# The sums of the second product: who forms them, and in which order the seven products run

## The chip, the cores and the metric

The kernel runs on one core of one Trainium2 chip. The metric is device time in microseconds (us), the median of 13 runs. A core has five engines that run side by side, each through its own queue in order: TensorE (PE in the profile; its weight loads are PEld), VectorE (DVE), ScalarE (ACT), GpSimd (POOL) and SyncE (SP), which here only issues DMAs. They wait for each other through semaphores. TensorE writes its results to PSUM, in banks of 128 x 512 float32.

## The reference

Two layers in a row. First an attention with masks: 8 batches, 8 heads, 576 positions, head size 64. Heads 0 to 3 see the last 32 positions, heads 4 to 7 every 32nd one. Its output, 4608 tokens of 512 numbers, goes through a feed-forward layer with a leaky activation:

```python
h = x @ w_in                       # 512 -> 2048
g = np.maximum(h, 0.0) + alpha * np.minimum(h, 0.0)
return (g @ w_out).astype(np.float32)   # 2048 -> 512
```

## The kernel before, in words

**Chunks.** The feed-forward part runs in 9 chunks of 512 tokens (`n` = 0 to 8, `NCH` = 9). The attention of batch n+1 is cut into pieces that are woven into chunk n: transposes of q and k (T), scores (S), the product with v (P, "pv"), and transposes of the result (X). Chunks 1 to 6 carry such pieces, 7 and 8 none. Everything is issued in an order written out by hand (`keep`), so an engine's queue is the order of the code.

**A chunk** has 30 slots (loop at L929). Slots 0 to 15 are the first layer: `lin1_piece` multiplies x by 128 columns of w_in (4 matmuls of 512 columns) into one of three PSUM banks (`hbank`), ScalarE forms the negative part (L647), and VectorE finishes the activation into `gT` (L650, called through the list `late` in the next attention step). A bank is free again once L650 has read it. The pieces alternate: 0, 8, 1, 9 and so on. Slots 16 to 29 are the second layer, `lin2_sums` with i = 0 to 13. After each slot `attn_n` issues as many attention pieces as an accumulator (`acc`) says.

**The second layer** of chunks 1 to 8 uses Strassen's scheme in Winograd's form. g (512 tokens x 2048) and w_out are cut into quadrants; in place of eight block products there are seven, of sums of quadrants. The sums of w_out (`wsum`, and one quadrant of `wout16` overwritten in place) are formed once by `w_sums` (L682). The sums of g are formed per chunk by `g_sum` (L696):

- g1 = quad(1,0) + quad(1,1); g2 = g1 - quad(0,0); g4 = quad(0,1) - g2; g3 = quad(0,0) - quad(1,0), written over quad(1,0) in place.

g1 is formed by GpSimd in three parts of 128 x 512 while the first layer runs (L933), its last part and all others by VectorE at i = 0, 1 and 2. quad(i, j) takes the tokens' half i and the rows 8j to 8j+7 of `gT`, so quad(0,0) and quad(1,0) need pieces 0 to 7 and the other two 8 to 15.

The seven products go into three banks A, B, C. Product p takes slots i = 2p and 2p + 1, one for each half of the tokens, with 8 matmuls of 256 columns in each. In order: A (quad(0,0)), B (g1), A (g2, added to what A holds), B (g4), A (g3), C (quad(0,1)), A (quad(1,1)). After some of them ScalarE copies a bank to SBUF (k1, k5, k2, L763) or VectorE adds a bank and such a copy (L766): o12 = B + k2 after the fourth, o22 = A + k5 after the fifth, o11 = C + k1 after the sixth; o21 is A after the seventh. Each is stored by a DMA on SP's queue (L714).

**Other queues.** GpSimd multiplies the masks into the scores (L427, L434), casts inputs (L196) and issues loads. SP issues stores, loads of q and k, and transposing DMAs: x to xT (L489, L487), and, once per batch, q and k of the strided heads (L141), which the scores of those heads wait for.

**Before chunk 1**, chunk 0's second layer is plain (`lin2_piece`, L664). At its slot 9 VectorE forms the first two sums of w_out and GpSimd the last; GpSimd forms the third after the loop (L694).

Of the kernel before, what the change touches and what calls it, by code (L numbers as in the profile page):

```python
# [9 lines left out]
F32 = mybir.dt.float32  # L10
F16 = mybir.dt.float16
# [20 lines left out]
def kernel(  # L32
# [10 lines left out]
    nc = tc.nc  # L43
# [4 lines left out]
    NCH = NT // 512  # L48
# [5 lines left out]
    cpool = ctx.enter_context(tc.tile_pool(name="const", bufs=1))  # L54
    spool = ctx.enter_context(tc.tile_pool(name="stage", bufs=3))
# [26 lines left out]
    win16 = cpool.tile([128, 4, 2048], F16)  # L82
    wout16 = cpool.tile([128, 16, 512], F16)
    xT = cpool.tile([128, 4, RING], F16)
    gsum = [cpool.tile([128, 8, 256], F16, name=f"gsum{i}") for i in range(3)]
    wsum = [cpool.tile([128, 8, 256], F16, name=f"wsum{i}") for i in range(3)]
    banks = [phpool.tile([128, 512], F32, tag=f"hb{i}", name=f"hb{i}") for i in range(3)]
    turn, busy = [0, 1], []
# [585 lines left out]
    def quad(t, i, j):  # L674

        return t[:, 8 * j : 8 * j + 8, 256 * i : 256 * i + 256]

    def wq(i, j):

        return wout16[:, 8 * i : 8 * i + 8, 256 * j : 256 * j + 256]  # L680

    def w_sums(eng, which):  # L682

        w1, w2, w4 = wsum
        w3 = wq(0, 1)
        steps = {
            1: (w1, wq(0, 1), wq(0, 0), ALU.subtract),
            2: (w2, wq(1, 1), w1, ALU.subtract),
            3: (w3, wq(1, 1), wq(0, 1), ALU.subtract),
            4: (w4, wq(1, 0), w2, ALU.subtract),  # L690
        }
        for z in which:
            o, x, y, op = steps[z]
            keep(eng.tensor_tensor(o, x, y, op=op))  # L694

    def g_sum(eng, n, which, k0, k1):  # L696

        g = gTs[n]
        g1, g2, g4 = gsum
        g3 = quad(g, 1, 0)  # L700
        o, x, y, op = {
            1: (g1, quad(g, 1, 0), quad(g, 1, 1), ALU.add),
            2: (g2, g1, quad(g, 0, 0), ALU.subtract),
            3: (g3, quad(g, 0, 0), quad(g, 1, 0), ALU.subtract),
            4: (g4, quad(g, 0, 1), g2, ALU.subtract),
        }[which]
        keep(eng.tensor_tensor(o[:, k0:k1], x[:, k0:k1], y[:, k0:k1], op=op))  # L707
# [3 lines left out]
    def store(n, i, j, osb, mts=(0, 1)):  # L711
# [3 lines left out]
            out[r0 : r0 + 128 * len(mts), 256 * j : 256 * j + 256].rearrange("(m p) c -> p m c", p=128),  # L715
            osb[:, mts[0] : mts[-1] + 1]))

    def lin2_sums(n, i):

        g = gTs[n]  # L720
        last = n == NCH - 1
        p, mt = i // 2, i % 2
        if i == 0:
            tiles = [banks[z] for z in turn]
            lay.clear()
            for nm, t in zip("ABC", tiles):
                lay[nm] = [t[:, 0:256], t[:, 256:512]]
                lay[nm + "f"] = t
            turn[:] = [turn[1], turn[2], turn[0]]
            if last:  # L730
                lay["A"][1] = pspool.tile([128, 512], F32, tag="ps", name="opl")[:, 0:256]
            g_sum(nc.vector, n, 1, 6, 8)
            g_sum(nc.vector, n, 2, 0, 4)
            g_sum(nc.vector, n, 2, 4, 8)
        if i == 1:
            g_sum(nc.vector, n, 4, 0, 8)
        if i == 2:
            g_sum(nc.vector, n, 3, 0, 8)
        bank, lhs, rhs, first = (
            ("A", quad(g, 0, 0), wq(0, 0), True),  # L740
            ("B", gsum[0], wsum[0], True),
            ("A", gsum[1], wsum[1], False),
            ("B", gsum[2], wq(1, 1), False),
            ("A", quad(g, 1, 0), wq(0, 1), False),
            ("C", quad(g, 0, 1), wq(1, 0), True),
            ("A", quad(g, 1, 1), wsum[2], False),
        )[p]
        dst = lay[bank][mt]
        own = mt == 0 or (last and bank == "A")
        for kf in range(8):  # L750
            keep(nc.tensor.matmul(  # L751
                dst, lhs[:, kf, 128 * mt : 128 * mt + 128], rhs[:, kf, :],
                start=(first and own and kf == 0), stop=(kf == 7), skip_group_check=True))

        def each(fn, o, *more):

            if last and bank == "A":
                fn(o[:, mt], lay["A"][mt], *[z[:, mt] for z in more])
            elif mt == 1:
                fn(o, lay[bank + "f"].rearrange("p (m c) -> p m c", m=2), *more)  # L760

        def act(o, x):
            keep(nc.scalar.copy(o, x))  # L763

        def add(o, x, y):
            keep(nc.vector.tensor_tensor(o, x, y, op=ALU.add))  # L766

        def new(nm):
            if mt == 0:
                held[nm] = (kpool if nm[0] == "k" else opool).tile(  # L770
                    [128, 2, 256], F32, tag=nm if nm[0] == "k" else "osb", name=nm)
            return held[nm]

        if p == 0:
            each(act, new("k1"))
        elif p == 1:
            each(act, new("k5"))
        elif p == 2:
            each(act, new("k2"))
        elif p == 3:  # L780
            each(add, new("o12"), held["k2"])
            if mt:
                store(n, 0, 1, held["o12"])
        elif p == 4:
            each(add, new("o22"), held["k5"])
            if mt:
                store(n, 1, 1, held["o22"])
        elif p == 5:
            each(add, new("o11"), held["k1"])
            if mt:  # L790
                store(n, 0, 0, held["o11"])
        else:
            o21 = new("o21")
            if last and mt:
                keep(nc.vector.tensor_copy(o21[:, 1], lay["A"][1]))
            else:
                each(act, o21)
            if last:
                store(n, 1, 0, o21, (mt,))
            elif mt:  # L800
                store(n, 1, 0, o21)
# [14 lines left out]
            keep(nc.tensor.matmul(wps, wrm[:, 0:128], wrm, start=True, stop=True))  # L816


    wrm = cpool.tile([128, 512], F16)
    wps = banks[2]  # L820
    def load_unit(b, strided, v_too=True):
        load_qk(b, strided, "q")
# [87 lines left out]
        attn_n(0, end1)  # L910
    for i in range(16):
        lin2_piece(0, i)
        if i == 9:
            w_sums(nc.vector, (1, 2))
            w_sums(nc.gpsimd, (4,))
        attn_n(0 if i < 1 else 2 if i < 9 else 1, end1)
    while pos["i"] < end1:
        attn_step(end1)
    wide["on"] = False
    w_sums(nc.gpsimd, (3,))  # L920
    load_unit(3, False)


    for n in range(1, NCH):
        ab = attn_until(n + 1) if n + 1 < B else len(pieces)
        left = ab - pos["i"]
        skip = 4 if n == 1 else 0
        acc = 0.0
        for i in range(30):  # L929
            if i < 16:  # L930
                lin1_piece(n, 8 * (i % 2) + i // 2)
                if i in (3, 7, 11):
                    late.append(lambda i=i: g_sum(nc.gpsimd, n, 1, i // 2 - 1, i // 2 + 1))  # L933
            else:
                lin2_sums(n, i - 16)
            if i >= skip:
                acc += left / ((19 if n == B - 2 else 20.5) - 0.5 * skip) * (0.5 if i < 16 else 1.0)
            cnt = int(acc)
            acc -= cnt
            attn_n(cnt, ab)  # L940
        while pos["i"] < ab:
            attn_step(ab)
# [30 lines left out]
```

## Time and profile before

| | |
|---|---|
| median of 13 runs | 330.66 us (326.71 to 334.95) |
| profiled execution, its own time | 330.84 us |
| its span, first to last instruction | 329.0 us |
| granted TensorE clock | 0.99 |
| PE, DVE, ACT, POOL busy | 307.0, 232.3, 174.6, 181.4 us |
| g_sum on GpSimd (L707), 128x512 | 24 times, 1.15 us each |
| g_sum on VectorE, 128x512 / 128x1024 / 128x2048 | 0.43 / 0.68 / 1.21 us as a rule |
| w_sums (L694), 128x2048, VectorE / GpSimd | 1.21 / 4.05 us |

The page gives for each engine its busy time and its share of the span. Matmuls are pipelined, so their durations overlap: the time of a stretch is read from the start of one group to the start of the next. A row of the timeline has the start in us, the duration, the engine, the line of the code, the operation, output and inputs, how many, and in brackets the idle time before it and what ended it.

### The profile page before, as it was taken

How to read it: one execution, taken by the hardware profiler on the slowest of the kernel's cores; microseconds unless marked ns; L12 is line 12 of the kernel's file. 1: busy time of each engine (PE TensorE's matmuls, PEld its weight loads, DVE VectorE, ACT ScalarE, POOL GpSimd, SP SyncE). 2: the span in 40 equal slices, each digit the busy share in tenths (PEclk: the TensorE clock that was granted, in tenths of full speed). 3: DMA queues.
4: the chain of work that ended last, by engine and by line, in shares of the span. 5: the costliest groups of instructions: out<-in, count | busy, mean ns of one | idle time of the engine just before them, and what ended most of it. 6: DMA issues, size and time to landing. Idle time of an engine off the chain costs nothing.

```text
span 329.0 us, 7189 instructions
## 1 busy us (share of the span) xinstructions
PE 307.0 (93%) x2861; PEld 200.6 (61%) x2861; DVE 232.3 (71%) x420; ACT 174.6 (53%) x325; POOL 181.4 (55%) x180
## 2 busy tenths in 40 slices
PE   7699989999779999999999999999999999999995
PEld 2265446555457546854688878646864685486484
DVE  5356864757797688658875887488748995865872
ACT  1375655458434775377527753775367607624630
POOL 8672388198996975587558744974345401200400
PEclk9799999999899999999999999999999999999999
DMA  7999999949855997399729992997180122003003
GB/s 216 200 206 207 241 184 124 137 149 178 190 78 94 181 213 94 72 210 185 93 53 138 252 111 53 120 162 90 39 191 18 21 55 95 0 12 119 0 2 128
DMA packets 81569, 40.38 MB, mean 123 GB/s; under 512 B 58480, under 2 KB 77184, under 8 KB 81536
## 3 DMA queue, kind: packets, MB, share of 16 engines
q0 software_dynamic: 41728, 17.38, 47.3%
q1 hardware_dynamic: 39808, 22.55, 30.2%
q8 instruction: 22, 0.36, 0.5%
q14 instruction: 11, 0.09, 0.1%
HBM read 38.01 MB, written 9.44 MB: 144 GB/s over the span
## 4 chain that ended last, share of the span: by engine, by line
PE 51%; DVE 21%; DMA 12%; ACT 7%; issue 4%; POOL 2%; SPq 1%; ACTq 0%
PE hb L637 21%; PE hb L751 15%; DMA kT<-ksd 10%; DVE gT L650 6%; DVE gsum L707 5%; PE hb L664 4%; DMA kl<-in_k_dram 3%; DVE qT L194 2%; DVE x L464 2%; DVE gT L707 2%; PE pv L455 2%; ACT neg L647 2%; DVE x16s L464 2%; PE hb L816 2%; DVE rc L462 1%
## 5 line engine op out<-in xcount | busy, mean ns | idle before, releaser
L650 DVE SCALAR_TENSOR_TENSOR gT<-neg,oma,hb 128x512 f16<-128x512 f32 x144 | 105.3, 744 | 40.1 <-ACT neg L647 33.3
L637 PE MATMUL hb<-xT,win 128*128 128x512 f16 (+1 forms) x640 | 132.7, 358 | 0.7
L647 ACT ACTIVATE neg<-hb 128x512 f32<-128x512 f32 x144 | 86.0, 598 | 42.4 <-PE hb L637 40.5
L637 PEld LDWEIGHTS <-win 128*128 128x128 f16 x640 | 60.1, 98 | 56.3 <-issue 2.6
L707 POOL TENSOR_TENSOR gsum<-gT 128x512 f16<-128x512 f16 x24 | 27.7, 1153 | 63.9 <-DVE gT L650 63.6
L427 POOL TENSOR_TENSOR et<-et,consts 128x576 f16<-128x576 f16 (+1 forms) x24 | 31.9, 1331 | 39.6 <-ACT et L425 39.6
L751 PEld LDWEIGHTS <-gT 128*128 128x128 f16 x512 | 48.0, 99 | 9.1 <-DVE gT L650 1.6
L751 PE MATMUL hb<-wout,gT 128*128 128x256 f16 x368 | 47.6, 278 | 0.5
L751 PEld LDWEIGHTS <-gsum 128*128 128x128 f16 x384 | 35.6, 97 | 6.7 <-DVE gsum L707 1.9
L464 DVE TENSOR_TENSOR x<-pv,rc 96x384 f16<-96x384 f32 (+2 forms) x62 | 33.0, 532 | 2.1
L434 POOL TENSOR_TENSOR et<-et,consts 128x576 f16<-128x576 f16 (+1 forms) x24 | 31.4, 1309 | 0.7 <-ACT et L431 0.6
L751 PE MATMUL hb<-wsum,gsum 128*128 128x256 f16 x248 | 30.7, 273 | 1.2 <-DVE gsum L707 1.2
L455 PEld LDWEIGHTS <-et 72*128 72x128 f16 (+1 forms) x448 | 24.2, 98 | 11.2 <-POOL et L434 2.7
L462 DVE RECIPROCAL rc<-pv 72x6 f32<-72x6 f32 (+2 forms) x80 | 14.6, 182 | 22.5 <-PE pv L455 22.5
L766 DVE TENSOR_TENSOR o<-hb,k 128x512 f32<-128x512 f32 (+1 forms) x24 | 16.3, 679 | 15.4 <-PE hb L751 11.6
L425 ACT ACTIVATE et<-sp 128x576 f16<-128x576 f32 (+1 forms) x24 | 15.7, 652 | 21.3 <-PE sp L412 21.1
L763 ACT COPY k<-hb 128x512 f32<-128x512 f32 (+1 forms) x24 | 13.3, 572 | 21.4 <-PE hb L751 21.4
L431 ACT ACTIVATE et<-sph 128x288 f16<-128x288 f32 (+1 forms) x48 | 18.3, 413 | 0.9 <-PE sph L412 0.9
L816 PE MATMUL hb<-wrm 128*128 128x512 f16 x44 | 17.1, 466 | 1.2 <-DVE wrm L828 1.2
L751 PE MATMUL hb<-wout,gsum 128*128 128x256 f16 x128 | 16.2, 272 | 0.8 <-ACT k L763 0.8
L664 PE MATMUL hb<-wout,gT 128*128 128x512 f16 x64 | 16.3, 379 | 0.1
L455 PE MATMUL pv<-vs,et 72*128 72x65 f16 x256 | 15.4, 193 | 0.2 <-DVE x16s L464 0.2
(109 smaller groups left out, 339.4 us busy)
## 6 DMA issues: line engine op xcount, KB each, us to landing
out_dram<-o SPq DMA_DIRECT2D x31, 256.0 KB, 3.0
ql<-in_q_dram SPq DMA_DIRECT2D x6, 512.0 KB, 6.5
kl<-in_k_dram SPq DMA_DIRECT2D x6, 512.0 KB, 8.0
stv<-in_v_dram POOLq DMA_DIRECT2D x8, 288.0 KB, 7.5
vl<-in_v_dram POOLq DMA_DIRECT2D x6, 384.0 KB, 10.9
win<-in_moe_w_in_dram POOLq DMA_DIRECT2D x4, 512.0 KB, 9.3
wout<-in_moe_w_out_dram POOLq DMA_DIRECT2D x4, 512.0 KB, 13.3
qsd<-in_q_dram POOLq DMA_DIRECT2D x6, 288.0 KB, 5.8
```

The source lines that it names most:

```text
L427: keep(nc.gpsimd.tensor_tensor(mv, mv, m, op=ALU.mult))
L431: keep(nc.scalar.activation(ev[:, n * y : n * y + n], sps[y][0:r, 0:n], AF.Exp, scale=SCALE))
L434: keep(nc.gpsimd.tensor_tensor(mv, mv, m, op=ALU.mult))
L455: keep(nc.tensor.matmul(pv[:, 65 * x : 65 * x + 65], et[0:r, c : c + 128], v16[0:r, 2 * P.pr + hh, t, :] if P.strided else v16[:, 6 * (2 * ...
L464: keep(nc.vector.tensor_tensor(P.x16[0:w, c0 : c0 + 64 * nb].rearrange("r (c e) -> r c e", e=64), pvv[:, :, 0:64], rc[0:w, 0:nb].unsqueeze ...
L637: keep(nc.tensor.matmul(hps[:, dst : dst + w], win16[:, kk, 128 * m : 128 * m + 128], xT[:, kk, src : src + w], start=(kk == 0 and x == 0) ...
L647: keep(nc.scalar.activation(neg, hps, AF.Relu, scale=-1.0))
L650: keep(nc.vector.scalar_tensor_tensor(gTs[n][:, m, :], neg, oma[:, m : m + 1], hps, op0=ALU.mult, op1=ALU.add))
L664: keep(nc.tensor.matmul(ops, gTs[n][:, kf, 128 * mt : 128 * mt + 128], wout16[:, kf, :], start=(kf == 0), stop=(kf == 15)))
L707: keep(eng.tensor_tensor(o[:, k0:k1], x[:, k0:k1], y[:, k0:k1], op=op))
L751: keep(nc.tensor.matmul(dst, lhs[:, kf, 128 * mt : 128 * mt + 128], rhs[:, kf, :], start=(first and own and kf == 0), stop=(kf == 7), skip ...
L816: keep(nc.tensor.matmul(wps, wrm[:, 0:128], wrm, start=True, stop=True))
```

## The change

It has a function `quiet(n)`, true for chunks 7 and 8, which keep the old order. In chunks 1 to 6:

- lin1 pieces run in natural order 0 to 15.
- g3 gets a tile of its own (a fourth `gsum`) and is formed in lin1 slots 10 and 12, in two parts of 128 x 1024, by GpSimd (in chunk 1 by VectorE).
- g1 and g2 are each one VectorE instruction of 128 x 2048 at i = 0; g4 is one at i = 4.
- The product order is p = (0, 5, 1, 2, 3, 4, 6): the product into C comes second. Copies, adds and stores follow their product. The banks for the next chunk are handed over as C, B, A.
- If slot 27 would get no attention piece, it gets one.

For all chunks: weight sums 1, 2, 4 are on VectorE in slots 9, 11, 13 of chunk 0, and weight sum 3 on VectorE in lin1 slot 6 of chunk 1. To make room in SBUF, k1 shares k2's buffer (in chunks 7 and 8 the staging buffer of v), and the operand of the warm-up matmuls is a part of the first `gsum`.

```diff
@@ g_sum
-        g1, g2, g4 = gsum
-        g3 = quad(g, 1, 0)
+        g1, g2, g4, g3 = gsum
...
+    def quiet(n):
+        return n >= NCH - 2
@@ lin2_sums
-            turn[:] = [turn[1], turn[2], turn[0]]
+            turn[:] = [turn[1], turn[2], turn[0]] if quiet(n) else [turn[2], turn[1], turn[0]]
...
-            g_sum(nc.vector, n, 1, 6, 8)
-            g_sum(nc.vector, n, 2, 0, 4)
-            g_sum(nc.vector, n, 2, 4, 8)
-        if i == 1:
+            if quiet(n):
+                g_sum(nc.vector, n, 1, 6, 8)
+                g_sum(nc.vector, n, 2, 0, 4)
+                g_sum(nc.vector, n, 2, 4, 8)
+            else:
+                g_sum(nc.vector, n, 1, 0, 8)
+                g_sum(nc.vector, n, 2, 0, 8)
+        if i == (1 if quiet(n) else 4):
             g_sum(nc.vector, n, 4, 0, 8)
-        if i == 2:
+        if i == 2 and quiet(n):
             g_sum(nc.vector, n, 3, 0, 8)
+        p = (p if quiet(n) else (0, 5, 1, 2, 3, 4, 6)[p])
...
-            ("A", quad(g, 1, 0), wq(0, 1), False),
+            ("A", gsum[3], wq(0, 1), False),
...
+                if nm == "k1":
+                    pool, tag = (spool, "v") if quiet(n) else (kpool, "k2")
@@ chunk 0's second layer
-        if i == 9:
-            w_sums(nc.vector, (1, 2))
-            w_sums(nc.gpsimd, (4,))
+        if i in (9, 11, 13):
+            w_sums(nc.vector, ({9: 1, 11: 2, 13: 4}[i],))
...
-    w_sums(nc.gpsimd, (3,))
@@ the loop over chunks
-                lin1_piece(n, 8 * (i % 2) + i // 2)
-                if i in (3, 7, 11):
-                    late.append(lambda i=i: g_sum(nc.gpsimd, n, 1, i // 2 - 1, i // 2 + 1))
+                if quiet(n):
+                    lin1_piece(n, 8 * (i % 2) + i // 2)
+                    if i in (3, 7, 11):
+                        late.append(lambda i=i: g_sum(nc.gpsimd, n, 1, i // 2 - 1, i // 2 + 1))
+                else:
+                    lin1_piece(n, i)
+                    if i in (10, 12):
+                        g_sum(nc.vector if n == 1 else nc.gpsimd, n, 3, 2 * i - 20, 2 * i - 16)
+                if n == 1 and i == 6:
+                    w_sums(nc.vector, (3,))
...
+            if i == 27 and cnt == 0 and pos["i"] < ab:
+                cnt = 1
```

More of the change, by code (lines that the diff above doesn't have):

```diff
@@ L84 @@
     xT = cpool.tile([128, 4, RING], F16)
-    gsum = [cpool.tile([128, 8, 256], F16, name=f"gsum{i}") for i in range(3)]
+    gsum = [cpool.tile([128, 8, 256], F16, name=f"gsum{i}") for i in range(4)]
     wsum = [cpool.tile([128, 8, 256], F16, name=f"wsum{i}") for i in range(3)]
@@ L769, in new @@
             if mt == 0:
-                held[nm] = (kpool if nm[0] == "k" else opool).tile(
-                    [128, 2, 256], F32, tag=nm if nm[0] == "k" else "osb", name=nm)
+                pool, tag = (kpool, nm) if nm[0] == "k" else (opool, "osb")
+                if nm == "k1":
+                    pool, tag = (spool, "v") if quiet(n) else (kpool, "k2")
+                held[nm] = pool.tile([128, 2, 256], F32, tag=tag, name=nm, **({"bufs": 2} if tag == "v" else {}))
             return held[nm]
@@ L816, in warm @@
             keep(nc.tensor.matmul(wps, wrm[:, 0:128], wrm, start=True, stop=True))
-    wrm = cpool.tile([128, 512], F16)
+    wrm = gsum[0].rearrange("p k c -> p (k c)")[:, 0:512]
     wps = banks[2]
```

## The prediction

> **What bounds the kernel now.** I read the engine totals, then the busy time by stage, then the order of work in one stage.
>
> ```profile
> span 329.0 us, 7189 instructions
> PE 307.0 (93%) x2861; PEld 200.6 (61%) x2861; DVE 232.3 (71%) x420; ACT 174.6 (53%) x325; POOL 181.4 (55%) x180
> ...
> 69.00:115.20 46.20, 40.55 (x404) 25.69 (x403) 35.07 (x57) 26.46 (x51) 41.53 (x37) 0.96 0.90 150
> 115.20:148.37 33.17, 31.92 (x317) 21.14 (x316) 24.50 (x46) 19.45 (x37) 22.08 (x21) 1.00 1.03 149
> 148.37:181.74 33.37, 31.95 (x335) 23.08 (x336) 24.92 (x48) 19.47 (x37) 22.30 (x22) 1.00 0.87 120
> ```
>
> The stage rows give length, then PE, PEld, DVE, ACT and POOL busy. TensorE is the bound and the change takes no matmul away, so only its stalls can be won or added. Chunks 2 to 5 take 33.4 us each. Chunk 1 (68.5 to 109.7 in the order of TensorE's work) takes 41.2, with DVE and POOL both loaded. Next, TensorE in chunk 3's second layer, from its first product (slot 0) on:
>
> ```profile
> 159.13 1.35 PE L751 MATMUL hb<-wout,gT 128*128 128x256 f16 x8
> ...
> 162.69 0.61 PE L252 MATMUL tp<-consts,kl 128*128 128x128 f16 x8
> 163.65 0.27 PE L282 MATMUL tt<-consts,tl 128*128 128x128 f16 x2 [0.34 <-DVE qT L194]
> ...
> 166.73 0.58 PE L412 MATMUL sph<-qT,kT 64*128 64x96 f16 x6
> 167.51 1.03 PE L751 MATMUL hb<-wout,gsum 128*128 128x256 f16 x8 [0.20 <-ACT k L763]
> ...
> 172.83 1.05 PE L751 MATMUL hb<-wout,gT 128*128 128x256 f16 x8
> 173.72 0.35 PE L455 MATMUL pv<-vl,et 128*128 128x65 f16 x6
> 173.90 1.04 PE L751 MATMUL hb<-wsum,gT 128*128 128x256 f16 x8
> ...
> 181.30 0.30 PE L412 MATMUL sp<-qT,kT 64*128 64x72 f16 x8 [0.37 <-DMA kT<-ksd]
> ```
>
> A slot's eight matmuls take 0.87 us from start to start. Stalls: 0.3 at slot 0 (waits for gT), 0.5 at the transposes of a tail (the qT copy on DVE is late), 0.55 at the scores after slot 5, 0.37 at the scores that wait for a transposing DMA. VectorE in the same stretch, and in chunk 1:
>
> ```profile
> 160.83 0.43 DVE L707 TENSOR_TENSOR gsum<-gT 128x512 f16<-128x512 f16 x1
> 161.17 1.29 DVE L707 TENSOR_TENSOR gsum<-gsum,gT 128x1024 f16<-128x1024 f16 x2
> 162.37 1.22 DVE L194 COPY qT<-tp 128x1024 f16<-128x1024 f16 x1
> ...
> 173.92 0.69 DVE L766 TENSOR_TENSOR o<-hb,k 128x512 f32<-128x512 f32 x1 [1.52 <-PE hb L751]
> ...
> 88.83 4.32 DVE L707 TENSOR_TENSOR gsum<-gT 128x512 f16<-128x512 f16 x1
> ```
>
> **What the Trainium skill says.** "SBUF — State Buffer", Who interferes with whom: a VectorE instruction with two SBUF inputs and a GpSimd instruction that reads SBUF exclude each other for a whole instruction. The trace agrees: the sum at 88.83 took 4.32 us instead of 0.43, while GpSimd ran masks and casts without a gap to 92.8. "PSUM — Partial Sum Buffer", PSUM bank collisions: two engines may not touch one bank together, so work is ordered by bank. The trace agrees in the tail's bank: ScalarE's kT copy waited 2.36 us for VectorE's qT copy. "GPSIMD Engine Reference", Engine selection: two-input work is about 2 times slower on GpSimd; here 2048 elements take 4.05 against 1.21 us, and that is used.
>
> **Part 1: the turn from the fifth product to the last (slots 10, 11 to 12, 13).** Both use bank A. Before, product C stood between them; now it is second. After slot 11, o22 = A + k5 must be read by VectorE before TensorE writes A again. The last row of TensorE's slot 11 shows the price: matmuls from 172.83, the add at 173.92 for 0.69, so A is free at 174.61, about 174.66 with the 0.05 us of other handovers. TensorE is ready at 173.90. Only the pv piece (0.19) stands between, and it is already in that 173.90. Stall 0.76. It covers the 0.15 us that the next transposes wait for today: +0.6 a chunk in 2 to 5, +0.75 in chunks 1 and 6. The rule at i == 27 adds nothing: by the same accumulator every chunk from 1 to 6 already has a piece in that slot, so attention pieces stay where they are.
>
> **Part 2: start of layer 2, chunks 2 to 5.** Lin1 in natural order makes gT 0 to 7 ready early: slot 0's 0.3 goes. But g1 is now whole on VectorE: two sums of 1.13 (spacing of a 2048-element sum) plus 0.1 stand ahead of the qT copy, 2.4 us instead of 1.6. That copy ends near 164.4, not 163.59, and the tail's transposes wait for its buffer: 0.8 later, and since TensorE arrives 0.3 earlier its wait grows from 0.5 to some 1.5. Then it is given back: g4 leaves slot 1 and g3 leaves VectorE, so the tail copies, which waited behind them until 166.46, are done by 165.1, and the 0.55 at the scores is gone. Following both engines' queues, slot 6 begins at 167.6 instead of 167.51: +0.15 with rounding (bounds -0.4 and +0.6). The second product covers the new g1 and g2, which end at 163.2; they are needed at 165.3 and 167.6. k1 shares k2's buffer: read at slot 3, written again at slot 7.
>
> **Part 3: g3 on GpSimd.** 512 elements cost 1.15, 2048 cost 4.05, so 1024 about 2.1, twice, against 3 x 1.15 before: +0.8 a chunk on an engine busy 22 of 33. Queued behind it: two DMA issues (now ahead of it, 2 us earlier) and the masks of the scores in slot 12. In chunk 3 the masks end at 160.3 instead of 160.0; g1 begins at 160.82. Cost nothing while that 0.5 us margin holds.
>
> **Part 4: SP's queue.** The store of o12 stood ahead of the qT and kT transposing DMAs at 170.42; now o11's, done at slot 3, does, and the transposes start about 1.7 us earlier. Their stalls, 0.45, 0.20, 0.37 and 0.43 in chunks 2 to 5, go: -1.45 in all. The loads of tails and v behind the old weight sums on GpSimd start up to 10 us earlier; nothing waited for them.
>
> **Part 5: chunk 1.** Weight sums 1, 2, 4 on VectorE in slots 9, 11, 13 of chunk 0: 3 x 1.21, hidden, since VectorE idles 1.46 and 1.90 us there. The third, at i == 6, stands ahead of a finish that frees a bank (three banks): +0.75. g3 there is 2 x 0.68 on VectorE beside a GpSimd that runs without a gap from 79.6 to 86.1: nothing if it slips in, 3 us if it starves as at 88.83; I take +0.25. GpSimd's 8.1 us of weight sums were over by 72.3 and it waited 0.72 for ScalarE at 79.6, so the 2.25 us stall for its mask at 86.16 stays. In layer 2 the slot-0 stall of 0.8 goes, but g1 and g2 must still find the lock free: 0.8 later to 0.5 earlier at the tail's transposes; with the gain spent I take the two together as -0.75. Turn +0.75. Sum 0.75 + 0.25 - 0.75 + 0.75 = +1.0, bounds -3.3 and +3.
>
> **Part 6: chunk 6.** No tail. VectorE's sums meet GpSimd's masks (259.71 to 262.4) today and would again; g4, queued after the pv copies, ends near 267.65 for a slot that starts at 267.57: +0.1, and the turn +0.75. Chunks 7 and 8 keep their order; g3 out of place costs the same.
>
> **Sum.** 4 x (0.6 + 0.15) - 1.45 + 1.0 + 0.85 = +3.4 us on the profiled 330.84 (span 329.0, 1.8 around it). The median of the runs is 330.66, so 334.1.
>
> **Rivals.**
> - Not slower: chunk 1's lock stall vanishes, because the order of POOL and DVE there is new. Between 87.86 and 100.38 TensorE spends 12.5 us on 8.2 of work (by starts: seven slots of 0.87, four pv of 0.19, scores 0.36, transposes 0.45 and 0.56); all 4.3 won gives 334.1 - 4.3 = 329.8. It decides once g1 starts at once instead of after 3.9 us. For it: POOL has one sum of 1.15 less there. Against: the masks and casts that held the lock remain.
> - The turn is cheaper: an attention piece runs long or VectorE answers sooner, 0.3 instead of 0.76: -2.7, 331.4. Against: the piece there is 0.19.
> - Masks late in every chunk: GpSimd's sums take 0.5 longer than interpolated, g1 meets the lock and all of layer 2 moves by 1 us in four chunks: 338.
> - The edits don't act (i == 27 indeed does not): excluded for the order of products, which is written out.
>
> **How the numbers follow.** 0.5 for the forecast (332.3 to 336.5), 0.22 for chunk 1's relief (half of it, with other gains, below 329.0), 0.10 for the cheap turn, 0.10 for late masks, 0.08 for relief and cheap turn together (327.5). A difference under 0.5%, 1.65 us, is no change that can be told. Faster 0.11 + 0.08, same 0.11 + 0.10, slower 0.6. Range 328.0 to 338.0; the forecast's own stands above.
>
> **What would show it.** Right: a wait for the add of o22 before the last product in chunks 1 to 6, 0.6 to 0.8 each; no wait for kT's DMA after chunk 1; no 0.3 at slot 0; the tail's transposes waiting about 1.5. Wrong: chunk 1 under 39 us, waits at the turn under 0.4, or a first sum of several us in chunks 2 to 5.

## The result, and the profile after

The changed kernel takes 337.45 us (median of 11 runs, 335.45 to 341.93) against 330.71 (48 runs): 1.0221 of the time before, 95% interval 1.0185 to 1.0258. It is slower, as forecast, but by 6.7 us where 3.4 were forecast. The ratios here and below leave out executions more than 1.5% above the fastest of their kernel; the medians do not.

The head of the page of the changed kernel, and its busy time by chunk (length; then busy time of PE, PEld, DVE, ACT, POOL, each with its instructions; then TensorE's granted clock, DMA share, GB/s):

```profile
span 338.5 us, 7176 instructions
PE 308.5 (91%) x2861; PEld 202.6 (60%) x2861; DVE 240.0 (71%) x412; ACT 174.5 (52%) x325; POOL 173.8 (51%) x170
...
70.94:118.59 47.65, 37.12 (x364) 24.09 (x363) 38.79 (x51) 23.04 (x44) 25.55 (x25) 0.89 0.71 124
118.59:151.82 33.23, 31.41 (x317) 21.14 (x315) 24.61 (x44) 19.45 (x36) 24.58 (x22) 1.00 1.02 145
```

The same rows of the kernel before:

```profile
68.50:109.67 41.17, 35.97 (x364) 23.56 (x363) 31.41 (x50) 23.14 (x44) 37.00 (x32) 0.96 0.86 143
109.67:143.07 33.40, 31.90 (x317) 21.11 (x315) 24.75 (x46) 19.46 (x36) 23.61 (x24) 1.00 1.02 139
```

Chunk 1 grew by 6.5 us, with 7.4 us more of VectorE and 11.5 us less of GpSimd; chunk 2 did not grow. By the starts of TensorE's groups, the chunks compare so (us):

| | before | changed |
|---|---|---|
| start of chunk 1 | 68.48 | 70.94 |
| chunk 1 | 41.19 | 47.65 |
| chunks 2, 3, 4, 5 | 33.40, 33.15, 33.41, 33.38 | 33.23, 33.23, 33.73, 33.23 |
| chunk 6 | 30.19 | 30.70 |
| chunk 7 | 26.06 | 26.06 |

The start of chunk 1 lay anywhere from 64.6 to 72.3 us in the profiled executions of this study, with the same TensorE work before it; so below chunks are compared, not whole profiled times. Each figure by chunk comes from one profiled execution. That of the changed kernel took 340.30 us at a granted clock of 0.97, longer than its median; that of the kernel before took 330.84 at 0.99. From chunk 1 on the profiled execution lost 338.5 - 70.94 less 329.0 - 68.48, which is 7.0 us: 6.5 in chunk 1, 0.1 in chunks 2 to 5 together, 0.5 in chunk 6.

**Where chunk 1 lost it.** (L706, L759, L771 and L774 of the changed kernel are L707, L751, L763 and L766 of the one printed above.) TensorE's timeline in chunk 1 of the changed kernel: the wait for a mask in slot 14, the one for a finish (L650) in slot 15, and the one inside the scores of pair 11, the last two heads of batch 2, whose scores stand behind slot 18 in the second layer:

```profile
89.88 0.36 PE L455 MATMUL pv<-vl,et 128*128 128x65 f16 x6 [2.62 <-POOL et L434]
94.95 1.86 PE L637 MATMUL hb<-xT,win 128*128 128x512 f16 x4 [4.71 <-DVE gT L650]
...
103.38 0.30 PE L412 MATMUL sph<-qT,kT 64*128 64x72 f16 x7 [1.12 <-DVE x L464]
```

What VectorE did then (finishes, then a g3 part, and so on):

```profile
82.92 1.74 DVE L706 TENSOR_TENSOR gsum<-gT 128x1024 f16<-128x1024 f16 x1
84.58 1.39 DVE L650 SCALAR_TENSOR_TENSOR gT<-neg,oma,hb 128x512 f16<-128x512 f32 x2
85.90 7.65 DVE L706 TENSOR_TENSOR gsum<-gT 128x1024 f16<-128x1024 f16 x1
...
98.26 2.15 DVE L706 TENSOR_TENSOR gsum<-gT 128x2048 f16<-128x2048 f16 x1
100.45 2.18 DVE L706 TENSOR_TENSOR gsum<-gsum,gT 128x2048 f16<-128x2048 f16 x1
```

And GpSimd in the same time:

```profile
84.07 2.47 POOL L196 COPY vs<-stv 72x1024 f16<-72x1024 f16 x2
86.48 0.81 POOL L176 DMA_DIRECT2D stv<-in_v_dram  x1
87.31 1.29 POOL L427 TENSOR_TENSOR et<-et,consts 128x576 f16<-128x576 f16 x1
88.55 1.27 POOL L434 TENSOR_TENSOR et<-et,consts 128x576 f16<-128x576 f16 x1
89.76 1.04 POOL L196 CAST ql<-ql 128x1024 f16<-128x1024 f32 x1
90.77 1.26 POOL L434 TENSOR_TENSOR et<-et,consts 128x576 f16<-128x576 f16 x1
91.98 1.03 POOL L196 CAST kl<-kl 128x1024 f16<-128x1024 f32 x1
98.06 1.27 POOL L427 TENSOR_TENSOR et<-et,consts 72x576 f16<-72x576 f16 x1 [5.06 <-ACT et L425]
```

The second half of g3, 0.68 us of work, took 7.65: it began at 85.90 and ended at 93.5, just after GpSimd had run out of work at 93.0. Its inputs had been ready since about 81. The finishes behind it kept TensorE's banks, hence the 4.71. In two other runs with the same sums, turn_apart and c1_warm below, the same instruction took 7.66 and 7.65. The two sums of the second layer then took 2.15 and 2.18 instead of 1.21, each beside a mask.

**Where chunk 3 moved.** TensorE in chunk 3, from the tail's transposes to the next chunk's scores, which used to wait for kT's DMA:

```profile
172.57 0.27 PE L282 MATMUL tt<-consts,tl 128*128 128x128 f16 x2 [1.10 <-ACT kT L192]
...
182.10 0.35 PE L455 MATMUL pv<-vl,et 128*128 128x65 f16 x6
183.05 1.03 PE L759 MATMUL hb<-wsum,gT 128*128 128x256 f16 x8 [0.60 <-DVE o L774]
...
189.70 0.30 PE L412 MATMUL sp<-qT,kT 64*128 64x72 f16 x8
```

VectorE:

```profile
169.31 1.23 DVE L706 TENSOR_TENSOR gsum<-gT 128x2048 f16<-128x2048 f16 x1
170.57 1.23 DVE L706 TENSOR_TENSOR gsum<-gsum,gT 128x2048 f16<-128x2048 f16 x1
171.72 1.22 DVE L194 COPY qT<-tp 128x1024 f16<-128x1024 f16 x1
...
182.30 0.69 DVE L774 TENSOR_TENSOR o<-hb,k 128x512 f32<-128x512 f32 x1 [1.47 <-PE hb L759]
```

The wait before the last product is there, in all six chunks (0.60 five times, 0.52 once, by the page's waits of TensorE). The tail's transposes wait longer than before, and the scores at 189.70 wait no more. With no mask near, the sums take 1.23.

### The profile page after: what moved, and what is told of

It is laid out like the page before. It is cut to its first block, busy times and chain, and to the rows that moved or that the text cites. A ratio compares the mean times of both kernels' runs of the same rounds, so it can differ in the third digit from the quotient of the medians.

```text
span 338.5 us, 7176 instructions
## 1 busy us (share of the span) xinstructions
PE 308.5 (91%) x2861; PEld 202.6 (60%) x2861; DVE 240.0 (71%) x412; ACT 174.5 (52%) x325; POOL 173.8 (51%) x170
## 4 chain that ended last, share of the span: by engine, by line
PE 69%; DVE 19%; ACT 6%; issue 3%; DMA 2%; SPq 0%; ACTq 0%; DVEq 0%
PE hb L637 27%; PE hb L759 24%; DVE gsum L706 6%; DVE gT L650 5%; PE hb L664 4%; PE pv L455 3%; DMA kl<-in_k_dram 2%; PE hb L826 2%; DVE x L464 2%; DVE o L774 2%; ACT neg L647 2%; PE tp L252 1%; DVE qT L194 1%; PE sp L412 1%; ACT kT L192 1%
## 5 line engine op out<-in xcount | busy, mean ns | idle before, releaser
L650 DVE SCALAR_TENSOR_TENSOR gT<-neg,oma,hb 128x512 f16<-128x512 f32 x144 | 105.3, 744 | 40.3 <-ACT neg L647 33.2
L647 ACT ACTIVATE neg<-hb 128x512 f32<-128x512 f32 x144 | 86.0, 597 | 48.2 <-PE hb L637 47.9
L759 PEld LDWEIGHTS <-gsum 128*128 128x128 f16 x512 | 47.4, 98 | 6.6 <-DVE gsum L706 0.8
L706 POOL TENSOR_TENSOR gsum<-gT 128x1024 f16<-128x1024 f16 (+1 forms) x16 | 28.0, 1765 | 43.0 <-DVE gT L650 43.0
L759 PEld LDWEIGHTS <-gT 128*128 128x128 f16 x384 | 36.5, 99 | 9.9 <-issue 4.1
L434 POOL TENSOR_TENSOR et<-et,consts 128x576 f16<-128x576 f16 (+1 forms) x24 | 32.4, 1350 | 0.9 <-ACT et L431 0.9
L759 PE MATMUL hb<-wout,gT 128*128 128x256 f16 x248 | 32.8, 280 | 0.0
L759 PE MATMUL hb<-wsum,gsum 128*128 128x256 f16 x248 | 31.0, 273 | 0.0
L759 PE MATMUL hb<-wout,gsum 128*128 128x256 f16 x248 | 30.2, 273 | 0.7 <-DVE gsum L706 0.7
L771 ACT COPY k<-hb 128x512 f32<-128x512 f32 (+1 forms) x24 | 13.6, 569 | 32.8 <-PE hb L759 32.8
L774 DVE TENSOR_TENSOR o<-hb,k 128x512 f32<-128x512 f32 (+1 forms) x24 | 16.3, 680 | 16.9 <-PE hb L759 12.7
L706 DVE TENSOR_TENSOR gsum<-gT 128x2048 f16<-128x2048 f16 (+2 forms) x12 | 21.9, 1824 | 0.3
L826 PE MATMUL hb<-gsum 128*128 128x512 f16 x44 | 18.1, 485 | 1.2 <-DVE gsum L838 1.2
L759 PE MATMUL hb<-wsum,gT 128*128 128x256 f16 x120 | 15.2, 272 | 3.5 <-DVE o L774 3.5
```

Source lines behind the costliest of these rows:

```text
L434: keep(nc.gpsimd.tensor_tensor(mv, mv, m, op=ALU.mult))
L647: keep(nc.scalar.activation(neg, hps, AF.Relu, scale=-1.0))
L650: keep(nc.vector.scalar_tensor_tensor(gTs[n][:, m, :], neg, oma[:, m : m + 1], hps, op0=ALU.mult, op1=ALU.add))
L759: keep(nc.tensor.matmul(dst, lhs[:, kf, 128 * mt : 128 * mt + 128], rhs[:, kf, :], start=(first and own and kf == 0), stop=(kf == 7), skip ...
```

## The experiments

**The theories.** Lock: a VectorE sum with two inputs in SBUF cannot run beside a GpSimd instruction that reads SBUF, and in chunk 1 GpSimd's masks and casts leave it no gap; so what counts is which VectorE sums stand where GpSimd is busy. Load: VectorE has 2.6 us more of sums in chunk 1's first layer, wherever they stand. Turn: the loss is the six waits before the last product. Later runs added two questions: what the low clock costs, and what the order of products does to chunk 1.

All ratios are against runs of the kernel before on the same chip, with 95% intervals. This table holds what the traces show of chunk 1 (us). "Over" is the time that VectorE's sums there took beyond 0.43, 0.68 and 1.21 us for 512, 1024 and 2048 elements; "scores" is when TensorE resumed the scores of pair 11, from the chunk's start, and "rest" what came after; "half clock" is the time at a granted clock of 0.5. Each row is one profiled execution.

| kernel | chunk 1 | over | scores | rest | half clock | chunks 2 to 5, mean | chunk 6 |
|---|---|---|---|---|---|---|---|
| before | 41.2 | 4.2 | 26.6 | 14.6 | 3.4 | 33.3 | 30.2 |
| changed | 47.7 | 9.9 | 32.4 | 15.2 | 10.2 | 33.4 | 30.7 |
| c1_g3_early | 46.5 | 4.3 | 29.2 | 17.4 | 6.8 | 33.6 | 30.7 |
| c1_g3_pool | 50.3 | 5.4 | 32.8 | 17.4 | 13.7 | 33.4 | 30.7 |
| turn_apart | 46.9 | 10.0 | 32.4 | 14.5 | 6.8 | 33.0 | 30.9 |
| wsums_alone | 42.0 | 3.9 | 27.4 | 14.6 | 3.4 | 33.4 | 30.2 |
| c1_casts_act | 44.0 | 3.8 | 27.7 | 16.2 | 6.8 | 33.4 | 30.7 |
| c1_warm | 48.2 | 9.9 | 32.0 | 16.2 | 6.8 | 33.4 | 30.7 |
| c1_old_sums | 45.4 | 5.2 | 29.2 | 16.2 | 6.8 | 33.4 | 30.7 |
| both | 43.8 | 5.0 | 28.4 | 15.4 | 6.8 | 33.1 | 30.9 |
| after_vcast | 41.8 | 3.8 | 25.6 | 16.2 | 3.4 | 33.4 | 30.7 |
| before_vcast | 43.4 | 5.9 | 27.6 | 15.9 | 6.8 | 33.3 | 30.2 |
| both2 | 41.9 | 4.1 | 26.6 | 15.3 | 3.4 | 32.9 | 30.9 |
| both2_vcast | 40.0 | 3.9 | 24.1 | 15.9 | 3.4 | 32.9 | 30.9 |
| c1_undone | 42.7 | 3.9 | 27.4 | 15.3 | 3.4 | 33.4 | 30.7 |
| best | 40.5 | 3.9 | 24.1 | 16.4 | 6.8 | 32.9 | 30.1 |

### g3 of chunk 1 ahead of the masks: c1_g3_early

```diff
-                    if i in (10, 12):
-                        g_sum(nc.vector if n == 1 else nc.gpsimd, n, 3, 2 * i - 20, 2 * i - 16)
+                    at = (4, 8) if n == 1 else (10, 12)
+                    if i in at:
+                        k0 = 4 * at.index(i)
+                        g_sum(nc.vector if n == 1 else nc.gpsimd, n, 3, k0, k0 + 4)
```

> The changed kernel, but in chunk 1 the two g3 sums on VectorE are issued in first-layer slots 4 and 8 instead of 10 and 12, ahead of GpSimd's masks; the amount of VectorE work is the same. Lock theory: the second g3 (7.65 us in the changed kernel) falls to about 0.7 us, TensorE's 4.7 us wait in slot 15 vanishes with the low clock after it, chunk 1 takes 41 to 43 us instead of 47.6, and the time is 1.003 to 1.008 of the kernel before. Load theory (VectorE's added 2.6 us of sums is what delays the finishes, wherever they stand): chunk 1 stays at 46 or more, 1.02. Turn theory (the six waits before the last product are the loss): no change, 1.02.

1.0132 (1.0102 to 1.0162). Both g3 parts took 0.69 us and the wait of slot 15 was gone, as the lock theory said. But chunk 1 still took 46.5, not 41 to 43, and 46 or more is what the load theory had forecast. What speaks against load is where the time went. VectorE and then TensorE in its second layer:

```profile
90.18 4.01 DVE L706 TENSOR_TENSOR gsum<-gT 128x2048 f16<-128x2048 f16 x1
94.23 2.71 DVE L706 TENSOR_TENSOR gsum<-gsum,gT 128x2048 f16<-128x2048 f16 x1
```
```profile
92.26 0.20 PE L412 MATMUL sph<-qT,kT 64*128 64x72 f16 x1
97.69 0.42 PE L412 MATMUL sph<-qT,kT 64*128 64x72 f16 x7 [5.23 <-DVE x L464]
98.04 1.89 PE L759 MATMUL hb<-wout,gT 128*128 128x256 f16 x8
```

The lockout had moved on to g1 and g2. Behind them in VectorE's queue stand the copies of pv that free the scores' PSUM buffers, so TensorE stood 5.23 us in one piece. After that its clock was 0.5 from 96.8 to 103.6, and eight matmuls took 1.68 us from start to start instead of 0.87. So a part of the lock theory's forecast failed: to move one sum out of the way is not enough.

### g3 of chunk 1 on GpSimd: c1_g3_pool

```diff
-                        g_sum(nc.vector if n == 1 else nc.gpsimd, n, 3, 2 * i - 20, 2 * i - 16)
+                        g_sum(nc.gpsimd, n, 3, 2 * i - 20, 2 * i - 16)
```

> The changed kernel, but in chunk 1 g3 is formed by GpSimd in slots 10 and 12 as in the other chunks. Lock theory: VectorE no longer starves in the first layer, so the 4.7 us wait goes; but 2.1 us of sum now stand ahead of the mask that TensorE waits for in slot 14, so that wait grows from 2.6 to about 4.7, and the clock falls after it: chunk 1 43.5 to 46 us, 1.010 to 1.016 of before. Load theory: VectorE loses 1.4 us of work, chunk 1 about 46, 1.018. Turn theory: 1.02.

1.0315 (1.0224 to 1.0406): worse than the changed kernel. The wait for the mask in slot 14 grew to 4.37, as expected, but GpSimd's longer run then locked g1 and g2 out: "over" 5.4, a second wait of 5.16 at the scores, and the half clock twice.

### Bank A never twice in a row: turn_apart

```diff
-        p = (p if quiet(n) else (0, 5, 1, 2, 3, 4, 6)[p])
+        p = (p if quiet(n) else (0, 5, 2, 1, 4, 3, 6)[p])
```

> The changed kernel with the products in the order (0, 5, 2, 1, 4, 3, 6), so that two products into bank A never follow each other; chunk 1 is left as it is. Turn theory: the 0.75 us wait before the last product goes in chunks 1 to 6 (4.5 us): 1.008 of before. Lock theory: the turn costs what the trace shows, 0.6 to 0.75 a chunk less what other engines hold back anyway, so 3 to 4 us: 1.009 to 1.013; chunk 1 keeps its 4.7 us wait. If the wait only moves elsewhere (g2 is now wanted two slots earlier): no change, 1.02.

1.0184 (1.0119 to 1.0248). In the trace the waits before the last product are gone, chunks 3 to 5 take 0.45 us less each (32.78, 33.28, 32.78 against 33.23, 33.73, 33.23), chunk 2 0.14 less, and chunk 6 0.2 more. That is 1.3 us in chunks 2 to 6, not 3 to 4: the wait costs 0.45 a chunk where it costs anything. Chunk 1 keeps its 4.72 us wait. The turn theory falls as the main cause. The interval is too wide to confirm 1.3 us by time alone.

### The weight sums alone: wsums_alone

An edit of the kernel before:

```diff
-        if i == 9:
-            w_sums(nc.vector, (1, 2))
-            w_sums(nc.gpsimd, (4,))
+        if i in (9, 11, 13):
+            w_sums(nc.vector, ({9: 1, 11: 2, 13: 4}[i],))
...
-    w_sums(nc.gpsimd, (3,))
...
+                if n == 1 and i == 6:
+                    w_sums(nc.vector, (3,))
```

> The kernel before with the move of the weight sums alone: 1, 2 and 4 on VectorE in slots 9, 11, 13 of chunk 0, 3 on VectorE in slot 6 of chunk 1. Lock theory: only the finish behind the third sum is late, +0.6 us, and GpSimd's freed 8.1 us are worth nothing: 0.999 to 1.004 of before. Load theory: the 1.2 us on VectorE in chunk 1's first layer delay all later finishes: 1.005 or more. Relief theory (GpSimd's 8.1 us were holding the masks back): 0.993 or less.

1.0029 (0.9993 to 1.0066). TensorE waits 0.62 for a finish in slot 9, chunk 1 is 0.8 longer, and the 2.25 us wait for the mask stays. The 8.1 us taken off GpSimd are worth nothing there.

### GpSimd's casts of chunk 1 on ScalarE: c1_casts_act

```diff
-                        cast_l(b, pr)
+                        cast_l(b, pr, "act" if b == 3 else "pool")
...
-                    cast_v(b, pr, "pool")
+                    cast_v(b, pr, "act" if b == 2 else "pool")
```

> The changed kernel, but the four casts that GpSimd makes between its masks in chunk 1 (v of batch 2, q and k of batch 3) are made by ScalarE; VectorE's queue is the same. Lock theory: GpSimd's runs without a gap get shorter, VectorE's two-input sums in chunk 1 wait 5 us in all or less instead of about 10, chunk 1 takes 42.5 to 45 us instead of 47.6, 1.008 to 1.016 of before. Load theory (VectorE's own work): chunk 1 stays at 46.5 or more, 1.02.

1.0102 (0.9954 to 1.0251); by the trace chunk 1 is 3.7 us shorter than in the changed kernel. VectorE's queue is the same; its sums in chunk 1, by form (minimum, median, maximum in ns):

```profile
L706 DVE TENSOR_TENSOR gsum<-gT x3: 1525/1743/2146, 80.1 to 90.8; 128x1024 f16<-128x1024 f16 x2, 128x2048 f16<-128x2048 f16 x1
```

The longest is 2.15 us where it was 7.65, and "over" falls from 9.9 to 3.8. So the 7.65 was neither VectorE's load nor its inputs: it came from what GpSimd ran beside it. ScalarE's casts cost something too (a wait of 1.85 for an exponential).

### TensorE kept busy: c1_warm

18 matmuls that nothing reads, ahead of the piece of slot 15:

```diff
+                    if n == 1 and i == 15:
+                        wt = pspool.tile([128, 512], F32, tag="ps", name="wt")
+                        for _ in range(18):
+                            keep(nc.tensor.matmul(wt, win16[:, 0, 0:128], win16[:, 0, 0:512], start=True, stop=True))
                     lin1_piece(n, i)
```

> The changed kernel with 18 matmuls of 512 columns that nobody reads (3.9 us at full clock) in front of chunk 1's last first-layer piece, where TensorE waits 4.7 us. Clock theory: part of the loss in chunk 1 is the half clock that follows a long wait; TensorE stays busy, the clock holds at 1.0 from there to the scores, and chunk 1 takes 44.5 to 46 us, 1.011 to 1.018 of before. If the low clock costs nothing of its own (the other engines set the pace there): chunk 1 47 to 48.5, 1.02 to 1.025.

1.0323 (1.0209 to 1.0437), chunk 1 48.2: the clock theory's forecast missed, and chunk 1 lies where the other branch had put it, 47 to 48.5 (the time, 1.02 to 1.025, does not). The clock did recover: slots 0 to 2 ran at 0.87 us each. But TensorE then came to the scores of pair 11 early and waited 2.83 us there for VectorE, and a second stretch of half clock followed. The scores were resumed at 32.0 instead of 32.4. What sets chunk 1 to that point is VectorE and GpSimd, not TensorE's clock; only the half clock after it costs. In the changed kernel the 10.2 us of half clock lay before that point, about 90.2 to 100.4; TensorE was busy for 5.79 us between 90.00 and 100.50, so by an estimate from these figures some 2.9 were lost at half speed; that most of it was hidden behind VectorE and GpSimd follows from the 32.0 against 32.4.

### Chunk 1 with the old sums: c1_old_sums

`oldsums(n)` takes the place of `quiet(n)` where the sums at i = 0, 1, 2 and the first layer's pieces are chosen:

```diff
+    def oldsums(n):
+        return quiet(n) or n == 1
```

> The changed kernel, but chunk 1 forms its sums as before: first-layer pieces in the order 0, 8, 1, 9, g1 for three quarters on GpSimd, g1's rest, g2, g4 and g3 on VectorE at i = 0, 0, 1, 2. The new order of products and the third weight sum in slot 6 stay. Lock theory: chunk 1 goes back to 41.5 to 43 us, and with the other chunks even the whole is 1.000 to 1.006 of before. If the new order of products is what hurts chunk 1: chunk 1 45 or more, 1.015 to 1.02.

1.0243 (1.0122 to 1.0364), chunk 1 45.4: the lock theory's forecast missed, and chunk 1 came out as forecast if the order of products is what hurts. With the sums as before, chunk 1 differs from the kernel before only in the order of products, the weight sum in slot 6 and the buffers of g3 and k1. VectorE and GpSimd where it was lost:

```profile
95.92 3.09 DVE L706 TENSOR_TENSOR gsum<-gsum,gT 128x1024 f16<-128x1024 f16 x2
```
```profile
97.16 1.29 POOL L427 TENSOR_TENSOR et<-et,consts 72x576 f16<-72x576 f16 x1
```

g2's two halves took 3.09 us; in the kernel before they took 1.28. With the product into C second, TensorE no longer waits for g1 in slot 3 and comes to the scores of pair 11 earlier. Their mask reaches GpSimd before VectorE's second half of g2 and locks it out. One wait of 4.24 us takes the place of two of 1.0 and 1.24.

### Both repairs: both

c1_old_sums with the order of turn_apart, and the last weight sum in slot 0:

```diff
-        p = (p if quiet(n) else (0, 5, 1, 2, 3, 4, 6)[p])
+        p = (p if quiet(n) else (0, 5, 2, 1, 4, 3, 6)[p])
...
-                if n == 1 and i == 6:
+                if n == 1 and i == 0:
                     w_sums(nc.vector, (3,))
```

> As the run with chunk 1's old sums, and with the products in the order (0, 5, 2, 1, 4, 3, 6) and the third weight sum in slot 0 of chunk 1, where VectorE idles. Lock and turn theory together: chunk 1 40.5 to 42 us, chunks 2 to 5 32.8 us each against 33.3 before, chunk 6 30.9 against 30.2: 1 to 2.5 us faster than before, 0.992 to 0.997. If chunk 1's losses are not in its sums: 1.005 or more.

1.0098 (1.0055 to 1.0140). The weight sum in slot 0 costs no wait any more, and chunks 3 to 5 are as in turn_apart; but chunk 1 is 43.8, with the same single wait (4.25) at the scores.

### The casts of v moved ahead: after_vcast and before_vcast

The same edit in the changed kernel and in the kernel before:

```diff
-        todo = [(c, pr) for pr in range(2)] if g % 4 == 0 and 8 <= g < npair else []
+        todo = [(c, pr) for pr in range(2)] if g % 4 == 0 and 12 <= g < npair else []
+        if g == 7:
+            todo = [(2, pr) for pr in range(2)]
```

> The changed kernel, but GpSimd's two casts of v for batch 2 and the load behind them are issued with the transposes ahead of chunk 1's first scores, where GpSimd idles, and not between its masks. VectorE's queue is the same. Lock theory: the mask that TensorE waits for in slot 14 comes about 2.8 us earlier, so that wait (2.6) goes, and VectorE's sums wait less for GpSimd: chunk 1 takes 41.5 to 44.5 us instead of 47.6, 1.003 to 1.013 of before. If VectorE's sums starve as before under the masks alone: chunk 1 45 to 47, 1.015 to 1.02.

0.9999 (0.9960 to 1.0038) of the kernel before, from 1.0221. Chunk 1 takes 41.8: 5.9 of its 6.5 us are won back with two GpSimd casts moved, no VectorE instruction touched. "Over" is 3.8. VectorE's two g3 parts, and GpSimd in the same time:

```profile
78.48 1.75 DVE L708 TENSOR_TENSOR gsum<-gT 128x1024 f16<-128x1024 f16 x1
81.46 1.67 DVE L708 TENSOR_TENSOR gsum<-gT 128x1024 f16<-128x1024 f16 x1
```
```profile
78.40 2.95 POOL L427 TENSOR_TENSOR et<-et,consts 128x576 f16<-128x576 f16 x2 [9.07 <-ACT et L425]
81.31 1.27 POOL L434 TENSOR_TENSOR et<-et,consts 128x576 f16<-128x576 f16 x1
82.53 1.50 POOL L196 CAST ql<-ql 128x1024 f16<-128x1024 f32 x1
```

GpSimd went on without a gap to 86.25 here too, yet each g3 part got in after one mask, and the mask or cast behind it waited. So a run without a gap can lock a sum out for its whole length, but need not.

> The kernel before with the same move of the two casts of v. Lock theory: the 2.25 us wait of slot 14 shrinks to 0.5 or less and the half clock after it (1.7 us) goes: chunk 1 37 to 39.5 us instead of 41.2, 0.986 to 0.994 of before. If that wait is set by ScalarE and not by GpSimd: no change, 0.998 to 1.003.

1.0126 (1.0072 to 1.0181): slower, against the forecast. Its four executions ran at low granted clocks, 0.973 to 0.983, so a part of that belongs to the half clock (last section); chunk 1 took 43.4. The mask's wait did shrink, to 0.37. But TensorE came to the scores earlier, and their masks met g2:

```profile
90.74 4.54 DVE L709 TENSOR_TENSOR gsum<-gsum,gT 128x1024 f16<-128x1024 f16 x2
```

So the move by itself is no gain; it repairs the changed kernel because there VectorE had a g3 in the way of that run.

### The order of products in chunk 1: both2 and both2_vcast

```diff
-        p = (p if quiet(n) else (0, 5, 2, 1, 4, 3, 6)[p])
+        p = (p if quiet(n) else ((0, 1, 5, 2, 3, 4, 6) if n == 1 else (0, 5, 2, 1, 4, 3, 6))[p])
```

> As the run called both, but chunk 1 takes the products in the order (0, 1, 5, 2, 3, 4, 6), so that TensorE again needs g1 before it comes to the scores of slot 2. If the order of products in chunk 1 lets TensorE run ahead, so that the scores' masks come before VectorE's second sum and lock it out (2.5 us there with old sums and new order): chunk 1 41 to 42.5 us instead of 43.8, 0.994 to 1.002 of before. If the order has no part in it: 43.5 to 44, 1.008.

By the trace as expected: g2's halves are back at 1.28, the single wait is again one of 1.03 and one of 1.24, and chunk 1 takes 41.9. By time it was 1.0122 (1.0047 to 1.0196), from four runs. That is the clock of these runs and not the kernel: at granted clocks of 0.995, 0.984, 0.979 and 0.973 they took 328.37, 331.62, 334.39 and 334.72, and the kernel before, on the same chip, took 328.6, 331.6, 334.0 and 335.0 on average at 0.995, 0.984, 0.979 and 0.974.

> The run before this one with the move of the two casts of v as well: both savings together, chunk 1 37.5 to 40 us, chunks 2 to 5 32.8 each, 0.982 to 0.993 of before, faster than both kernels. If the savings overlap: 0.995 to 1.0.

Chunk 1 took 40.0, chunks 2 to 5 on average 32.9. The four runs gave 326.46 to 332.48, median 331.67, against a median of 330.57 before, so the times don't confirm the forecast. Three of them ran at 0.972 to 0.974 and took 331.5 to 332.5; the kernel before took 335.0 there.

### Chunk 1 alone set back, and the best combination: c1_undone and best

c1_undone is c1_old_sums with the order (0, 1, 5, 2, 3, 4, 6) in chunk 1 and (0, 5, 1, 2, 3, 4, 6) elsewhere. best is both2_vcast with chunk 6 in the old order (`quiet` from NCH - 3 on).

> The changed kernel with chunk 1 alone set back: its sums as before and the products there in the order (0, 1, 5, 2, 3, 4, 6), which lets TensorE wait for g1 as before; the third weight sum in slot 6 and everything in chunks 2 to 8 stay changed. If chunk 1 holds nearly all of the loss (by the trace 6.5 of it): chunk 1 42 to 43 us, the other chunks as in the changed kernel, 1.001 to 1.007 of before. If part of the loss lies outside what the profile of chunk 1 shows: 1.012 or more.

Chunk 1 takes 42.7, 5.0 us less than in the changed kernel, and all other chunks are the same to 0.01 us. By time 1.0131 (1.0034 to 1.0227), median 333.25 against 330.27; the trace from chunk 1 on says +2.2 us. The forecast's 1.007 lies inside the interval, but the point lies with the other branch, 1.012 or more. So the trace supports chunk 1 as the main part, and the times don't settle it.

> The run called both2_vcast with chunk 6 in its old order as well. If the savings by chunk add up: chunk 1 39.5 to 40.5 us, chunks 2 to 5 32.8, chunk 6 30.2, together 3 us under before, 0.988 to 0.996. If the lock takes them back in chunk 1: 0.998 or more.

0.9901 (0.9858 to 0.9943). From chunk 1 on it takes 258.1 us against 260.5, 2.4 us less where 3 were forecast. Chunk 6 is back at 30.1. The medians of all executions, 329.91 (22 runs) against 330.27 (27 runs), don't show the gain, since best spent more time at half clock: 11.2 us on average against 8.9. At an equal granted clock it is the faster one: 331.7 against 334.9 on average at 0.974, and 329.5 against 331.5 at 0.984.

## Why the prediction was right or wrong

**The step that failed is part 5, in its term for g3 in chunk 1**, "nothing if it slips in, 3 us if it starves as at 88.83; I take +0.25", and with it the bound of +3 for the chunk. Measured: the two parts took 1.74 and 7.65 instead of 0.68 each, 8.0 us over, and chunk 1 lost 6.5 us instead of 1.0. I had read the lockout of 3.9 us at 88.83 as the size of a lockout. It was what was left of GpSimd's run at that place, up to its last mask; behind that it only issued DMAs:

```profile
91.60 1.27 POOL L434 TENSOR_TENSOR et<-et,consts 72x576 f16<-72x576 f16 x1
92.82 0.78 POOL L134 DMA_DIRECT2D qsd<-in_q_dram  x1
```

In chunk 1's first layer of the changed kernel GpSimd ran from 84.07 to 93.0 without a gap, and the sum issued at 85.90 waited for the end of that. The rows for this reading were in the profile of before: the run without a gap that the prediction names, from 79.6 on, went on to the masks and casts of 88.83, 13 us in one piece. The Trainium skill ("SBUF — State Buffer", Summary: rules for kernel authors) says that the second one to issue blocks until the first finishes; here VectorE, issued at 85.90, also lost against five masks and casts that began after it, so one instruction is no bound. The runs c1_casts_act and after_vcast show the cause: with the casts on ScalarE, or two of them and the load behind them moved ahead, the same VectorE queue takes 44.0 and 41.8. The term is not the whole price of that place, though: in c1_g3_early g3 was out of the way, g1 and g2 waited instead, and chunk 1 took 46.5.

That the sum missed by only 3.6 us is luck in part: chunk 1 was 5.5 us dearer than forecast, and the other parts together 1.8 us cheaper. All signs that the prediction named for being right came out or nearly so (the tail's transposes waited 1.10 to 1.49 us for 1.5), and none of those for being wrong: they looked at the turn, at the DMA and at the start of layer 2, and none at the term that failed.

The rest of part 5: the third weight sum cost 0.6 as a wait and 0.8 in the chunk (taken: 0.75). The 2.25 us wait for the mask stayed, 2.6. The gain in slot 0 could not come, since the 0.8 that I had read there as a stall was no wait. In the kernel before, slot 0 of chunk 1 ran at half clock (0.50, the third figure from the end), 1.68 us from start to start, and TensorE waited for nothing:

```profile
87.50:88.50 1.00, 1.00 (x20) 0.71 (x15) 0.94 (x2) 1.00 (x3) 1.00 (x2) 0.50 0.34 55
```
```profile
87.86 1.89 PE L751 MATMUL hb<-wout,gT 128*128 128x256 f16 x8
```

In the changed kernel slots 0 and 1 ran at half clock again. The 4.3 us of the first rival contain this loss too.

**A cost that I had not put in the sum is the half clock.** It lasted 10.2 us of chunk 1 instead of 3.4; by TensorE's busy time in the chunk, 37.12 against 35.97, an estimate is that 1.1 us more were lost to it. c1_warm shows that it isn't the main cause: most of it stood where VectorE set the pace. The single runs say the same. At granted clocks of 0.984 and 0.985 the changed kernel took 336.2 us on average (seven runs) and the kernel before, in the comparisons above, 331.4 at 0.984 (nine runs). So some 4.8 us are lost at an equal clock, and the rest comes with more half clock.

**Part 1, the turn: right in mechanism.** In chunk 3 the slot could have begun at 182.29, behind the pv piece, and began at 183.05, with the add at 182.30 taking 0.69: 0.76, as forecast. (The profile's 0.60 is the idle time alone.) Its net cost was smaller, 0.45 a chunk and not 0.6: slots 6 to 13 of chunks 2 to 5 took 9.17 us instead of 8.71, and turn_apart won 0.45 back in chunks 3 to 5. The rule at i == 27 did nothing, as said.

**Part 2, the start of layer 2: its chain shows in chunk 4 alone.** There the tail's transposes waited 1.49 us for the qT copy behind the two sums, as forecast:

```profile
206.31 0.27 PE L282 MATMUL tt<-consts,tl 128*128 128x128 f16 x2 [1.49 <-DVE qT L194]
```

In chunks 2, 3 and 5 the row names ScalarE's kT copy and 1.10 us. In chunk 3 that copy ended at 172.52, while the qT copy (171.72, 1.22 us) was by the trace still running, so the transposes there did not wait for the qT copy; why, the runs don't show. The scores after slot 5 waited no more, and in chunk 3 slots 0 to 5 took 8.27 us (167.61 to 175.88) instead of 8.38 (159.13 to 167.51): -0.1, forecast +0.15. Chunk 4 is 0.5 longer than the three others.

**Part 3: right.** The two parts of g3 on GpSimd took 4.22 us together (forecast 2 x 2.1), and g1 met no lock in chunks 2 to 5.

**Part 4: right.** TensorE has no wait for kT's DMA left after chunk 1. With all terms, chunks 2 to 5 came to +0.1 us instead of +1.55, because the turn cost 1.8 instead of 2.4, the start of layer 2 about nothing instead of 0.6, and the first layers gave 1.7 instead of 1.45.

**Part 6: right in direction, +0.5 instead of +0.85**: a wait of 0.66 for g4 and one of 0.52 at the turn.

**The rivals.** That chunk 1's lock stall would vanish had its place right and its sign wrong: the new order there met more lock, not less. Late masks in every chunk did not occur. The cheap turn was partly so.

## What to carry to other kernels

Before moving a sum with both inputs in SBUF to VectorE, look at what GpSimd does at that moment, not at VectorE's share: beside a GpSimd that runs without a gap the sum can take as long as that run, and everything behind it in VectorE's queue with it. A wait removed on the way to such a place is not won: TensorE arrives earlier, its next request reaches GpSimd earlier, and that may lock out the very sum it needs (before_vcast, c1_old_sums). Two products into one bank, where VectorE reads the bank in between, want a product into another bank between them: by the traces turn_apart won 0.45 us in each of chunks 3 to 5 with it.

## What the runs showed of the hardware

The lockout is not settled instruction by instruction in turn: VectorE's sum at 85.90 lost against a DMA issue and five masks and casts that began after it, while the one at 82.92 got in after one mask, and in after_vcast so did the one at 81.46. DMA issues are not a gap for certain either. In the kernel before, the sums from 93.07 on ran at full speed beside two of them (92.82 to 94.31). In before_vcast the second half of g2 began at 92.4, beside DMA issues only (to 93.42), and ended at 95.28, behind the mask of 93.44. What decides that, these runs don't tell.

The half clock comes in whole units. In the sixteen profiled kernels its time in chunk 1 was 3.4, 6.8, 10.2 or 13.7 us, multiples of 3.41. The windows of the changed kernel around the long wait (the column after the five engines is the granted clock):

```profile
87.00:90.00 3.00, 0.38 (x6) 0.12 (x5) 3.00 (x1) 0.62 (x2) 2.99 (x4) 1.00 0.49 62
90.00:94.95 4.95, 0.24 (x6) 0.14 (x5) 4.92 (x5) 0.00 (x0) 3.00 (x3) 0.52 0.14 22
94.95:97.34 2.39, 2.39 (x20) 0.89 (x20) 1.92 (x4) 0.49 (x1) 0.00 (x0) 0.50 0.00 0
```

After a wait of 2.25 us it came on in the kernel before (at 87.4); after one of 2.29 it did not in c1_g3_early. The Trainium skill ("TensorE: Matmul & The Clock Gate", Part 1: The HAM clock gate) gives a window of 4096 cycles at 1.2 GHz, 3.41 us, that runs freely. The traces agree with the length; that the phase of the window decides whether a wait is caught would fit, and is not shown.

Half clock also goes with most of the difference between runs of one kernel. For each of the 114 executions of the kernel before that the comparisons hold, the granted clock gives an estimate of its time at half clock, 2 x (1 - clock) x span: 3.2 to 18.0 us. With each us of it the execution was 0.48 us longer (correlation 0.94). So a unit of 3.41 us costs about 1.6 us, and five units in place of one are most of the way from 325.4 to 335.8 us.
